# Decode attention on one core: result matmuls placed behind the next tile's first sums, and a first K load in three pieces

## The chip, the cores, the metric

The kernel runs on one core of one Trainium2 chip. The metric is device time in microseconds (us), lower is better; executions of one kernel lay within 0.35% of each other here, except in experiment 7 (0.8%). "V margin" below is my own measure: the time from the issue of a V load to the landing of the load ahead of it in the queue, with landings read from the completion records among the trace's DMA packets (the last of 16 per load). These records are grouped in order of time, which is right as long as the 16 DMA engines drift apart by less than a load lasts. For every whole tile that is so (at most 5.4 us apart in any run, of 19.3 us); for the last small pieces the grouping is rough, except for the very last landing.

## The reference

```python
B, H, Sq, Skv, Dh = 8, 32, 1, 4096, 128          # all bf16
scores = jnp.einsum('bhqd,bhkd->bhqk', q, k) * Dh ** -0.5
attn = softmax(scores, axis=-1)
return jnp.einsum('bhqk,bhkd->bhqd', attn, v)
```

One query per head, 256 heads, K and V of 268 MB each: every byte is read once.

## The kernel before

Eight heads make a tile: 128 partitions by 256 columns (C) by 128 (D), 8.39 MB of K and as much of V, 32 tiles (NT). VectorE multiplies K by the query in four quarters of 64 columns and halves the products once or twice; TensorE sums over what is left of D by matmuls with the identity; VectorE collects the sums as scores and finds the maximum; ScalarE makes the weights; TensorE multiplies them with V in a loop, and `result_of` picks each head's part. K and V share three slots.

```python
kv_pool = ctx.enter_context(tc.tile_pool(name="kv_pool", bufs=SLOTS))     # SLOTS = 3
...
cuts = {                                      # pieces of a load; otherwise one piece
    ("k", 0): [C // 2] * 2,
    ("k", NT - 3): [C // 2] * 2,
    ("k", NT - 2): [C // 2] * 2,
    ("k", NT - 1): [C // 4, C // 4, C // 2],
    ("v", NT - 1): [C // 2, C // 4, C // 8, C // 16, C // 32, LAST, LAST],
}
...                                           # load(): the queries' load follows the first piece of K
def width_of(t, u):
    return D // 4 if u >= NU // 2 and t < NT - 3 else D // 2
...
for t in range(NT):
    loop = 0 < t <= LT                        # LT = NT - 3
    ...
    product(t, 0, Q)                          # VectorE, first quarter
    sum_over_d(t, 0)                          # TensorE
    if t + 1 < NT:
        q_prep(t + 1)
    product(t, Q, 2 * Q)
    sum_over_d(t, 1)
    scores_of(t, 0)                           # VectorE waits here for the first sums
    product(t, 2 * Q, 3 * Q)
    sum_over_d(t, 2)
    scores_of(t, 1)
    ...
    product(t, 3 * Q, C)
    sum_over_d(t, 3)
    scores_of(t, 2)
    if loop:
        values_loop(t - 1)                    # TensorE, some 16 us
        load("k", t + 1)
        load("v", t)
    ...
    scores_of(t, 3)
    weights_of(t)
    ...
    if t > 0:
        copy_of(t - 1)                        # ScalarE, from PSUM
        ...
        if t % R == 0:
            norm_of(n)                        # 1 matmul in the program
        result_of(t - 1)                      # 4 matmuls, need copy_of
```

## Time and profile before

| | before |
|---|---|
| time, median of the runs beside the changed kernel | 1262.24 us (1260.06 to 1263.07) |
| span of the profiled run | 1260.2 us |
| busy: VectorE, TensorE | 83%, 61% |
| VectorE waiting for sums / for K | 106.0 / 72.6 us |

The timeline lists start, length, engine, line, operation, operands, and in brackets the idle time before it and its releaser. This is VectorE over one tile in the middle:

```profile
591.80 4.43 DVE L185 TENSOR_TENSOR kt<-kt,qb 128x8192 bf16<-128x8192 bf16 x1 [2.71 <-DMA kt<-in_k_dram]
...
607.23 0.69 DVE L217 TENSOR_REDUCE sc<-ps 128x64 f32<-128x512 f32 x1 [2.01 <-PE ps L205]
...
626.36 0.69 DVE L217 TENSOR_REDUCE sc<-ps 128x64 f32<-128x512 f32 x1 [1.35 <-PE ps L205]
```

"First sums" are those of a tile's first quarter, "last sums" those of its last. There are two waits that could give: 2.71 us for K, and 2.01 us for the first sums, which TensorE can start only when the loop of the tile before is over.

### The profile page before, as it was taken

Reading aid. Unit: us, or ns where it says so; the run is one execution under the profiler, and the core shown is the slowest. Engines: PE = TensorE matmul, PEld = TensorE weight load, DVE = VectorE, ACT = ScalarE, POOL = GpSimd, SP = SyncE. Lnnn points to the kernel's source line nnn. Section 1 sums busy time; section 2 is a strip of 40 time slices with the busy share of each in tenths; the row PEclk is TensorE's granted clock in tenths of the full one; section 3 lists DMA queues with packets and bytes.
Section 4 is the critical chain, followed back from the end, with each engine's and each line's share of the span. In section 5 each row is a group of like instructions: output and inputs, shape, how many; then the busy total and the mean of one; then the engine's idle time right before and its main releaser. Section 6 shows DMA issues by size and latency. Waiting matters only on the chain. (4 is left out here: it accounts for less than half of the span.)

```text
span 1260.2 us, 11027 instructions
## 1 busy us (share of the span) xinstructions
PE 765.0 (61%) x3067; PEld 287.5 (23%) x3067; DVE 1040.8 (83%) x588; ACT 170.6 (14%) x625; POOL 3.3 (0%) x18
## 2 busy tenths in 40 slices
PE   2265577555776556765567755577555776557756
PEld 0021222211222212222122221222212222212222
DVE  5997988889888888888898888987889888898793
ACT  0111011110111101111011111011110111101111
POOL 0000000000000000000000000000000000000000
PEclk9677887777887778877788777887777887778867
DMA  9999999999999999999999999999999999999997
GB/s 401 433 399 433 433 431 429 410 433 437 435 433 431 425 433 433 433 431 431 431 435 427 433 431 429 433 429 431 433 422 433 433 433 431 433 424 430 429 444 307
DMA packets 11433, 537.33 MB, mean 426 GB/s; under 512 B 1808, under 2 KB 2064, under 8 KB 2320
## 3 DMA queue, kind: packets, MB, share of 16 engines
q1 hardware_dynamic: 11072, 536.94, 99.1%
q8 instruction: 14, 0.23, 0.1%
q10 hardware_dynamic: 336, 0.07, 0.0%
q14 instruction: 11, 0.09, 0.0%
HBM read 536.94 MB, written 0.07 MB: 426 GB/s over the span
## 5 line engine op out<-in xcount | busy, mean ns | idle before, releaser
L185 DVE TENSOR_TENSOR kt<-kt,qb 128x8192 bf16<-128x8192 bf16 x128 | 565.2, 4416 | 84.0 <-DMA kt<-in_k_dram 72.6
L205 PE MATMUL ps<-kt,ident 128*128 128x512 bf16 x792 | 260.3, 479 | 420.1 <-DVE kt L193 370.1
L288 PE MATMUL av<-vt,w 128*32 x1740 | 425.4, 396 | 4.5
L188 DVE TENSOR_TENSOR kt<-kt 128x4096 bf16<-128x4096 bf16 x128 | 293.4, 2292 | 4.4
L288 PEld LDWEIGHTS av<-vt,w 128*32 x1740 | 172.9, 99 | 262.7 <-issue 120.8
L249 ACT ACTIVATE w<-sc,bias 128x256 bf16<-128x256 f32 x256 | 126.4, 494 | 655.4 <-DVE bias L240 655.4
L205 PEld LDWEIGHTS <-ident 128*128 128x128 bf16 x792 | 84.5, 113 | 570.8 <-issue 522.5
L217 DVE TENSOR_REDUCE sc<-ps 128x64 f32<-128x512 f32 x128 | 88.0, 687 | 106.0 <-PE ps L205 106.0
L193 DVE TENSOR_TENSOR kt<-kt 128x2048 bf16<-128x2048 bf16 x58 | 71.0, 1225 | 2.0
L344 ACT ACTIVATE comb<-av 32x512 bf16<-32x512 f32 (+1 forms) x32 | 18.7, 586 | 321.5 <-PEq L278 313.8
L274 PE MATMUL av<-vt,w 128*32 128x512 bf16 x116 | 47.3, 500 | 14.7 <-issue 13.4
L249 ACT ACTIVATION_READ_ACCUMULATOR w<-sc,bias 128x1 f32 x256 | 47.7, 186 | 0.0
L360 PE MATMUL op<-comb,pick 32*16 32x128 bf16 (+1 forms) x128 | 12.1, 213 | 26.0 <-ACT comb L344 26.0
L168 ACT ACTIVATE qg<-qh 8x128 bf16<-8x128 f32 x32 | 8.5, 266 | 99.5 <-PE qh L164 99.5
L274 PEld LDWEIGHTS av<-vt,w 128*32 128x32 bf16 x116 | 6.9, 100 | 55.3 <-issue 55.3
L360 PEld LDWEIGHTS <-pick 32*16 32x16 bf16 (+1 forms) x128 | 8.8, 83 | 33.0 <-issue 32.6
L316 PE MATMUL av<-vt,w 128*32 128x512 bf16 x191 | 15.7, 424 | 0.0
L164 PE MATMUL qh<-q_all,ident 128*8 128x128 bf16 x32 | 7.1, 221 | 13.1 <-DMA q_all<-in_q_dram 13.1
L229 DVE TENSOR_REDUCE pmax<-sc 128x1 f32<-128x256 f32 x32 | 13.5, 421 | 1.1
L170 PE MATMUL qp<-qg,heads 8*128 8x128 bf16 x32 | 6.8, 213 | 11.4 <-ACT qg L168 11.4
L172 ACT ACTIVATE qb<-qp 128x128 bf16<-128x128 f32 x32 | 8.9, 277 | 9.6 <-PE qp L170 9.6
L336 DVE RECIPROCAL rz<-zp 16x1 f32<-16x1 f32 x16 | 2.3, 147 | 7.7 <-PE zp L328 7.7
(29 smaller groups left out, 51.0 us busy)
## 6 DMA issues: line engine op xcount, KB each, us to landing
kt<-in_k_dram SPq DMA_DIRECT2D x7, 4096.0 KB, 21.1
kt<-in_k_dram SPq DMA_DIRECT2D x2, 2048.0 KB, 15.5
vt<-in_v_dram SPq DMA_DIRECT2D x1, 4096.0 KB, 32.1
vt<-in_v_dram SPq DMA_DIRECT2D x1, 2048.0 KB, 36.8
vt<-in_v_dram SPq DMA_DIRECT2D x1, 1024.0 KB, 38.4
vt<-in_v_dram SPq DMA_DIRECT2D x1, 512.0 KB, 39.2
vt<-in_v_dram SPq DMA_DIRECT2D x31, 24.2
kt<-in_k_dram SPq DMA_DIRECT2D x28, 26.6
```

Source lines behind the costliest of these rows:

```text
L185: nc.vector.tensor_tensor(out=part, in0=part, in1=qb[:].to_broadcast([P, MC, D]), op=ALU.mult)
L188: nc.vector.tensor_tensor(out=part[:, :, 0 : D // 2], in0=part[:, :, 0 : D // 2], in1=part[:, :, D // 2 : D], op=ALU.add,)
L193: nc.vector.tensor_tensor(out=part[:, :, 0 : D // 4], in0=part[:, :, 0 : D // 4], in1=part[:, :, D // 4 : D // 2], op=ALU.add,)
L205: nc.tensor.matmul(ps[:], lhsT=ident[:], rhs=kt[:, u * UC : (u + 1) * UC, s * DS : (s + 1) * DS], start=(s == 0), stop=(s == n - 1),)
L217: made = nc.vector.tensor_reduce(out=scs[t][:, u * UC : (u + 1) * UC], in_=sums.pop((t, u))[:], axis=AX.X, op=ALU.add)
L229: nc.vector.tensor_reduce(out=pmax[:], in_=sc[:], axis=AX.X, op=ALU.max)
L249: nc.scalar.activation(out=w[:, :, g, :], in_=sc_g, func=ACT.Exp, bias=bias[:, g : g + 1], scale=scale, accum_out=esum[:, t % R, g : g + 1],)
L274: pe.matmul(av, lhsT=wf[:, i * nw : (i + 1) * nw], rhs=vf[:, i * nv : (i + 1) * nv], **how)
L288: pe.matmul(av, lhsT=wf[:, bass.ds(ow + i * nw, nw)], rhs=vf[:, bass.ds(ov + i * nv, nv)], start=False, stop=False,)
L316: nc.tensor.matmul(avs[t][j * AG : (j + 1) * AG, :], lhsT=w[:, i, :, :], rhs=vt[:, c0 : c0 + CB, :], start=(i < TG), stop=(j not in group[ ...
L344: nc.scalar.activation(out=comb[0:n, :, :], in_=av[0:n, :, :], func=ACT.Copy)
L360: nc.tensor.matmul(ops[n][:], lhsT=pick[0:e, m, r, :], rhs=comb[0:e, m, :], start=(r == 0 and m == 0), stop=(r == R - 1 and m == CB - 1),)
```

## The change

Its intent: the first sums no longer stand behind ScalarE's copy and the results (c); VectorE starts earlier as the queries follow a smaller piece of K (a); and tile 0 needs fewer additions on VectorE (b).

```diff
-        ("k", 0): [C // 2] * 2,
+        ("k", 0): [C // 4, C // 4, C // 2],
@@ width_of
-        return D // 4 if u >= NU // 2 and t < NT - 3 else D // 2
+        return D // 4 if u >= NU // 2 and 0 < t < NT - 3 else D // 2
@@ after sum_over_d(t, 0)
+            if 0 < t - 1 <= LT:
+                if (t - 1) % R == 0:
+                    norm_of(n)
+                if t > 1:
+                    result_of(t - 2)
@@ end of the tile
-                if t % R == 0:
-                    norm_of(n)
-                result_of(t - 1)
+                if not loop:
+                    if t % R == 0:
+                        norm_of(n)
+                    result_of(t - 1)
```

## The prediction

> **What bounds the kernel now.** I read the page of the kernel before in this order: busy shares, the 40 slices, the queues; then the transfer queue's own timeline, a table of stages, VectorE's waits, and the timeline of one tile.
>
> ```profile
> PE 765.0 (61%) x3067; PEld 287.5 (23%) x3067; DVE 1040.8 (83%) x588; ACT 170.6 (14%) x625; POOL 3.3 (0%) x18
> ...
> DMA packets 11433, 537.33 MB, mean 426 GB/s; under 512 B 1808, under 2 KB 2064, under 8 KB 2320
> ```
>
> VectorE is busy 83%, but the kernel must read 537 MB, and the row of DMA digits on the page is 9 in every slice but the last. So the stream of loads is the first suspect, and the question is how near 426 GB/s is to its ceiling. The table of stages says it:
>
> ```profile
> 38.70:77.40 38.70, 11.04 (x26) 3.48 (x26) 36.97 (x20) 4.58 (x18) 0.00 (x0) 0.59 1.00 434
> 77.40:116.10 38.70, 24.07 (x94) 8.93 (x94) 32.63 (x19) 5.17 (x19) 0.00 (x0) 0.81 0.96 407
> 116.10:1122.30 1006.20, 630.67 (x2466) 237.76 (x2466) 844.93 (x480) 137.66 (x507) 0.00 (x0) 0.80 1.00 430
> 1122.30:1238.40 116.10, 73.75 (x308) 27.21 (x308) 99.13 (x55) 15.12 (x56) 0.00 (x0) 0.74 1.00 433
> 80.50:81.90 1.40, 0.95 (x3) 0.13 (x2) 0.91 (x2) 0.00 (x0) 0.00 (x0) 0.50 0.00 0
> ```
>
> The last column is GB/s. The best stretch reaches 434: one tile of 8.39 MB in 19.33 us, a K and a V tile in 38.67. There is one true hole (80.5 to 81.9, nothing moves), and the long middle runs at 430, not 434. At 434 from end to end the kernel would need 1237 us; everything the change can win lies in what is above that: start, hole, middle, tail.
>
> The transfer queue's timeline shows where the hole is from:
>
> ```profile
> 80.95 0.33 SPq L151 DMA_DIRECT2D vt<-in_v_dram  x1
> 97.69 0.33 SPq L151 DMA_DIRECT2D kt<-in_k_dram  x1
> 119.66 0.33 SPq L151 DMA_DIRECT2D vt<-in_v_dram  x1
> 136.57 0.33 SPq L151 DMA_DIRECT2D kt<-in_k_dram  x1
> ```
>
> There are three slots. V(t) reuses the slot of K(t), so it is issued when the last sum of K(t) is done; K(t+2) reuses V(t-1), so it is issued when the loop of tile t-1 ends. From the DMA packets of the trace (their completion records, in order of time) I took when each tile landed. V(1) is issued at 80.95; the tile before it had landed at 80.47: late, hence the hole. After that every V is issued 3.3 to 4.7 us before the previous tile lands, every K 5.5 to 7.5 us before.
>
> VectorE over the whole run, and around one V issue:
>
> ```profile
> DVE sc L217 <- PE ps L205: 106.0, 61, 4.5
> DVE kt L185 <- DMA kt<-in_k_dram: 72.6, 26, 3.9
> DVE kt L185 <- ACT qb L172: 11.4, 1, 11.4
> ```
>
> 26 tiles make VectorE wait for K, about 2.8 us each: the middle is bound by transfers, compute has slack. 31 of the 61 waits for sums are the fixed one at the end of a tile (1.35 us mostly); the others are what the change aims at.
>
> **What the Trainium skill says.** "DMA: Bandwidth & Descriptors", section "Where 436 GB/s comes from", gives 435.2 GB/s as the ceiling of the 16 ports; this trace agrees (434 in the best stages). The same page, "Latency and other measured facts", gives about 0.6 us from a hardware-generated issue to the first byte; here the first packet after the issue at 80.95 starts at 81.90, so 0.95 us, and the first 16 packets took 3.0 to 3.3 us each where others take 2.42. "Runtime: NRT & Kernel Launch", section "Instruction fetch mechanics", says that instructions are refilled in blocks of 16 KiB over DMA and that a taken branch can force a fetch; the trace has 14 transfers of 0.23 MB together on a queue of kind "instruction", about 1 us each on one of the 16 DMA engines. The change keeps loop and branches, so these stay. "TensorE: Matmul & The Clock Gate", section "What's actually happening", says the array runs at half clock after idling; the sums of a tile show it: eight take 3.3 to 3.6 us at PEclk 0.5, 1.90 us right behind a loop.
>
> **The change, part by part.**
>
> *(a) First K load in quarters.* The query tile is issued after the first piece of K. Now that piece is half (4.2 MB, landed at 12.37), the queries landed at 12.64, and VectorE begins at 14.31 (the 11.4 us wait above). With a quarter, half of the piece's 9.67 us of streaming goes: queries at about 7.8, VectorE at 9.4. Gain 4.8 us; cost one more issue of 0.4 us and, as with the quarters of the last K (4.90 + 4.90 against 9.71), 0.1 us of stream. The later half lands at 22.4, when VectorE wants it at about 23.3: no new wait.
>
> *(b) Tile 0 halved once.* Removes two additions of 1.23 us from VectorE (2.4) and adds eight matmuls; the last sum of tile 0 takes 3.4 instead of 1.86, so 1.5 comes back on the path. Net 0.9. Together tile 0 is done 5.7 to 6 us earlier: 40.7 instead of 46.7. But K(1) lands at 41.7 and is usable at 42.2, so tile 1 starts at about 42.4 instead of 48.55, its last sum is done at about 74.8 instead of 80.95, and V(1) is issued 5.6 us before K(2) lands instead of 0.5 late. The hole goes: that tile took 22.70 us instead of 19.33, of which 0.9 is an instruction fetch that stays. **Gain 2.4 us for all later landings.**
>
> *(c) Result and norm behind the first sums.* The order of the built program confirms it: after a loop now come 4 result matmuls (with a norm before them every second tile) and then 8 sums; in the changed kernel 8 sums, norm, 4 results. One tile in the trace:
>
> ```profile
> 96.92 0.61 PE L274 MATMUL av<-vt,w 128*32 128x512 bf16 x2
> 98.33 0.38 PE L360 MATMUL op<-comb,pick 32*16 32x128 bf16 x4 [0.81 <-ACT comb L344]
> 98.64 1.90 PE L205 MATMUL ps<-kt,ident 128*128 128x512 bf16 x8
> ```
>
> The sums start at 98.64 and could start at 97.6, as the loop is done: the copy by ACT (0.59), its semaphores and four matmuls (0.31) leave VectorE's path, 1.0 to 1.1 us per tile. Nothing is added: ACT's copy then lies beside the sums, and the results (0.4 us) come before sums that VectorE needs some 8 us later.
>
> In the middle this is not on the bound. It becomes margin: the wait for the first sums averages 1.7 us there; if they come 1.05 earlier the V load is issued 1.05 earlier, the next loop too, and the wait falls again until it is zero. So V margins rise from about 4.1 to 4.1 + 1.7 = 5.7 us or so. Does margin help? I compared, from the packets, the mean landing of the 16 engines from tile to tile: K tiles (margins 6 to 7.5) take 19.34, V tiles (margins 3.3 to 4.7) 19.6 on average and up to 20.5; in the first 5 us after a V issue packets are stretched by up to 1.8 us, after a K issue by nothing. The one V with a margin of 5.3 took 19.35. Summed over 26 V tiles that is about 6.5 us, in agreement with 430 against 434 over 1006 us (9 us, fetches included). If margin is the cause, most of it goes; I count **4.5 us**, as an estimate, since the slowest engine and not the mean decides and fetches still spread the engines.
>
> *(d) The tail.* From tile 29 on, K comes in halves, VectorE no longer waits for loads, and the chain that ended last runs from 1187 on through VectorE:
>
> ```profile
> 1187.73 0.59 ACT comb L344
> 1188.33 0.04 issue
> 1188.37 0.38 PE op L360 x4
> 1188.75 1.85 PE ps L205 x8
> ```
>
> Here (c) is direct: tiles 28, 29 and 30 give 1.0 to 1.1 each, 3.2 in all. But V(31) limits it: its last piece landed at 1254.12, two microseconds before the last value matmul was done (1256.3). With data alone as the bound, its second half of matmuls (4.7 us now, twelve of them one behind another) would end at about 1254.1. **Gain 2.2 us**; the 3.9 us of copy, result, scale and store after it stay.
>
> Sum: 2.4 + 4.5 + 2.2 = 9.1 us; 1262.1 - 9.1 = **1253.0 us**.
>
> **The rivals.**
> *The stretched packets have nothing to do with margin* (memory or instruction fetches): for it, fetches do lie in some slow tiles, and V issues always fall where ACT and TensorE start; against it, K issues are clean. Then only 2.4 + 2.2 are won: 1257.5.
> *The hole is merely moved*: a faster start gives the time back at the next wait, or the quarters cost more in the start than they give. Speaks against it: the stream is idle only there. Then only the tail is won: about 1260.
> *All stretch goes and the engines stay together*: 2.4 + 6.5 + 2.2, 1251; with part of the instruction fetches absorbed too, 1249.5.
> *A new wait*: the results now sit ahead of the query matmuls and the next sums; one scratch tile between copy and result, one PSUM tile for the result. All have a whole tile of slack; I give it 3%.
>
> **Range and chances.** 1253.0, with 1249.5 to 1257.5 from the second and third lines of the rivals. A gain over 2% needs under 1237, the time of the pure stream: 1%. Slower by 2%: 1%. Within 2%: 98%.
>
> **What would show it.** Right: VectorE's first product near 9.4; V(1) issued near 75 and no stage at 407; the wait for sums down from 106 to about 60 us or less, and the wait for K up by about as much; the middle at 432 to 434; the final chain no longer through VectorE's products of tile 30 but ending behind the last V pieces. Wrong: V margins of 5.5 us or more with the middle still at 430 (then stretch is not from late issue); or waits for sums unchanged; or a new wait of PE on the copy.

## The result

The changed kernel takes 1253.45 us (1253.05 to 1254.02, 4 runs) against 1262.24 us (4 runs): a ratio of 0.9933, 95% interval 0.9916 to 0.9951. All ratios here are formed from fast runs; they are not quite the ratios of the medians. It is 8.8 us faster and clear of noise.

The stages of the changed kernel, the same windows as before. The columns are the window and its length, busy time and number of instructions of TensorE, its weight loads, VectorE, ScalarE and GpSimd, then the granted clock, the DMA share and GB/s:

```profile
77.40:116.10 38.70, 24.83 (x97) 9.35 (x96) 32.64 (x18) 5.74 (x22) 0.00 (x0) 0.81 1.01 434
116.10:1122.30 1006.20, 627.52 (x2464) 235.01 (x2462) 847.57 (x476) 137.00 (x505) 0.00 (x0) 0.79 1.00 433
```

The stage with the hole went from 407 to 434, the middle from 430 to 433. The transfer queue's timeline:

```profile
75.37 0.33 SPq L151 DMA_DIRECT2D vt<-in_v_dram  x1
92.16 0.33 SPq L151 DMA_DIRECT2D kt<-in_k_dram  x1
113.44 0.33 SPq L151 DMA_DIRECT2D vt<-in_v_dram  x1
```

V(1) is issued at 75.37, 5.1 us ahead of the landing of K(2), instead of 0.5 late. VectorE's waits (us in total, times, longest):

```profile
DVE kt L185 <- DMA kt<-in_k_dram: 98.9, 22, 5.9
DVE sc L217 <- PE ps L205: 56.6, 34, 3.6
DVE kt L185 <- ACT stage L369: 17.4, 4, 4.4
...
DVE kt L185 <- ACT w L249: 4.2, 1, 4.2
```

The wait for sums lost 49 us. The wait before a tile's first product gained 48: the rows put down to ACT are of the same length as those for K and stand at the same instruction, and a wait for several semaphores is put down to the one that came last by the profile, so I count them as waits for K (98.9 + 17.4 + 4.2 = 120.5 against 72.6). In the middle the wait for the first sums is gone, and K alone is waited for:

```profile
586.26 4.42 DVE L185 TENSOR_TENSOR kt<-kt,qb 128x8192 bf16<-128x8192 bf16 x1 [4.42 <-DMA kt<-in_k_dram]
...
599.59 0.69 DVE L217 TENSOR_REDUCE sc<-ps 128x64 f32<-128x512 f32 x1
```

TensorE after a loop:

```profile
91.39 0.60 PE L274 MATMUL av<-vt,w 128*32 128x512 bf16 x2
92.19 1.89 PE L205 MATMUL ps<-kt,ident 128*128 128x512 bf16 x8 [0.19 <-PEq L278]
94.00 0.39 PE L360 MATMUL op<-comb,pick 32*16 32x128 bf16 x4
```

The sums start 0.80 us after the loop's last matmuls start, where they started 1.72 us after before: 0.92 us came off. And the chain that ended last now ends in loads:

```profile
1201.69 40.81 DMA vt<-in_v_dram
1242.50 0.04 issue
1242.54 5.49 PE av L316 x29
...
1248.11 0.60 ACT comb L344
```

Where the 8.3 us between the two spans (1260.2 and 1251.9) came from, by landings:

| | before | after | gained | forecast |
|---|---|---|---|---|
| start, to the landing of K(3) | 123.41 | 120.63 | 2.8 | 2.4 |
| middle, K(3) to V(27) | 994.55 | 990.35 | 4.2 | 4.5 |
| V(27) to the last piece of V(31) | 136.16 | 136.10 | 0.1 | 0 |
| last landing to the end of the span | 6.1 | 4.8 | 1.2 | 2.2 |

### The profile page after: what moved, and what is told of

Same layout as the page of the kernel before. It is cut to its first block, busy times and chain, and to the rows that moved or that the text cites. A ratio compares the mean times of both kernels' runs of the same rounds, so it can differ in the third digit from the quotient of the medians.

```text
span 1251.9 us, 11042 instructions
## 1 busy us (share of the span) xinstructions
PE 767.1 (61%) x3075; PEld 286.0 (23%) x3075; DVE 1036.0 (83%) x586; ACT 170.6 (14%) x625; POOL 3.3 (0%) x18
## 5 line engine op out<-in xcount | busy, mean ns | idle before, releaser
L185 DVE TENSOR_TENSOR kt<-kt,qb 128x8192 bf16<-128x8192 bf16 x128 | 565.3, 4416 | 127.2 <-DMA kt<-in_k_dram 98.9
L316 PEld LDWEIGHTS <-w 128*32 128x32 bf16 x191 | 6.8, 105 | 11.0 <-issue 7.2
```

The source lines that it names most:

```text
L185: nc.vector.tensor_tensor(out=part, in0=part, in1=qb[:].to_broadcast([P, MC, D]), op=ALU.mult)
L316: nc.tensor.matmul(avs[t][j * AG : (j + 1) * AG, :], lhsT=w[:, i, :, :], rhs=vt[:, c0 : c0 + CB, :], start=(i < TG), stop=(j not in group[ ...
```

## The experiments

Each time stands beside runs of the kernel before on the same chip, whose median was 1261.76 us for the first four, 1261.98 for the next four and 1262.11 for the last four. "Middle" is the time from the landing of K(3) to that of V(27), "period" the median time from one V issue to the next from V(2) on; both, like the margins, are of the profiled run. All twelve kernels gave correct results.

| | time us | ratio | V margin, median | period | middle |
|---|---|---|---|---|---|
| before | 1262.24 | 1 | 4.12 | 38.92 | 994.55 |
| changed | 1253.45 | 0.9933 | 5.67 | 38.76 | 990.35 |
| 1 order only | 1255.86 | 0.9952 | 5.69 | 38.70 | 990.21 |
| 2 start only | 1256.68 | 0.9958 | 4.30 | 38.90 | 991.06 |
| 3 without (b) | 1253.12 | 0.9932 | 5.68 | 38.75 | 990.39 |
| 4 margin another way | 1254.32 | 0.9942 | 6.93 | 38.69 | 989.68 |
| 5 1.2 us off the cycle | 1253.93 | 0.9938 | 4.44 | 38.74 | 990.50 |
| 10 1.6 us off the cycle | 1257.46 | 0.9960 | 4.08 | 38.77 | 993.60 |
| 6 2.4 us off the cycle | 1266.82 | 1.0041 | 3.73 | 39.01 | 1002.50 |
| 7 3.7 us off the cycle | 1281.65 | 1.0161 | 3.27 | 39.83 | 1015.04 |
| 8 1.2 us in the cycle | 1260.14 | 0.9985 | 4.37 | 39.03 | 995.87 |
| 9 changed, again | 1253.40 | 0.9929 | 5.70 | 38.76 | 990.33 |
| 11 tail groups | 1253.43 | 0.9930 | 5.69 | 38.74 | 990.37 |
| 12 tail pieces | 1253.72 | 0.9933 | 5.68 | 38.75 | 990.50 |

My theory going in was the prediction's: the middle is bound by the stream of loads, and it runs at 430 instead of 434 GB/s because V loads are issued only about 4 us ahead ("margin theory"). Rivals: the slow packets are unrelated to margin; the start gives everything.

### 1. Only the order

The kernel before with part (c) alone; the edit is the last two hunks of the diff above.

> Only the new place of the result and norm matmuls; start as before. My theory (the hole is from the start, the stretched packets in the middle from V loads issued only about 4 us ahead, the tail from the last V pieces): the hole at 80 us stays, V(1) issued near 80.9; the wait for first sums goes to about zero after a few tiles and V margins rise to 5.6 us, the middle goes from 430 to 433 GB/s; end gains 4.5 (middle) + 1.3 (tail) = about 5.8 us, 1256.5 us, ratio about 0.9955. Rival (stretch has nothing to do with margin, the 7 us came from the start): only the tail is gained, 1.3 to 2 us, about 1260.5 us, ratio 0.9988.

Measured: 1255.86 us, 5.9 us gained where 5.8 were expected. V(1) is still issued at 80.91, the hole stays, and the middle is as in the changed kernel (990.21). The rival without a role for margin (1260.5) is out.

### 2. Only the start

```diff
-        ("k", 0): [C // 2] * 2,
+        ("k", 0): [C // 4, C // 4, C // 2],
-        return D // 4 if u >= NU // 2 and t < NT - 3 else D // 2
+        return D // 4 if u >= NU // 2 and 0 < t < NT - 3 else D // 2
```

> Only the start: first K in quarter, quarter, half, and tile 0 halved once; results stay ahead of the sums. My theory: V(1) issued near 75.4 as in the changed kernel, hole gone, 2.4 us gained; from tile 2 on V margins fall back to about 4 us because the first sums are late again, so the middle stays at 430 GB/s: about 1259.8 us, ratio 0.998. Rival (start gives it all): about 1255 us, ratio 0.994. Second rival (the gain is given back): 1262, ratio 1.000.

Measured: 1256.68 us. That is 5.1 us gained, twice what my theory gave, and with the 5.9 of the first experiment it makes more than both together give (8.8). The V issues show why, here V(3) and V(7):

```profile
153.44 0.33 SPq L151 DMA_DIRECT2D vt<-in_v_dram  x1
...
309.29 0.33 SPq L151 DMA_DIRECT2D vt<-in_v_dram  x1
```

The four steps average 38.96 us, as in the kernel before (38.97 over 25 steps), while the loads ahead of them landed every 38.76 us (159.04 to 314.09): hardly anything was stretched and the margin was comfortable. So in the order of before something else beats at 38.9 us: a cycle. The loop waits for the last sums of tile t, these for the second half of VectorE's work, that for the collected first sums, these for the first sums on TensorE, and those, in that order, for results, copy and the loop of the tile before. A K that lands earlier doesn't shorten it. The better start gave a head start: the margin was 5.6 us at V(3) and fell, in steps of 0.1 to 0.4 with one rise, to 3.7 us at V(13). The V issues kept it all: from V(1) to V(28) they lie 5.2 to 6.0 us before those of the kernel before. The landings caught up with them while the stream ran clean: 2.2 us earlier at V(1), 5.2 us at V(10). That is where the unexpected 2.7 us came from. It is also why the two parts overlap: with (c) the stream and no longer the cycle sets the pace, and a head start is then worth only what it saves the stream (2.8 us).

From here on I had a second theory, the "cycle theory": the cycle alone made the middle slow, and small margins were only its trace.

### 3. Without the halving of tile 0

The changed kernel with `t < NT - 3` restored in `width_of`.

> The changed kernel with tile 0 halved twice in its second half as before (so without part b). My working: tile 0 is done 0.6 to 0.9 us later, V(1) issued near 76, still over 4 us before K(2) lands, so no hole and later margins the same: time equal to the changed kernel within 0.3 us, 1253.5 us, ratio 0.993. If part b had carried the gain at the start: 1255 or more.

Measured: 1253.12 us, the same. V(1) is issued at 76.17 instead of 75.37 and still 4.3 us ahead. Part (b) does what it should, 0.8 us, and buys nothing once (a) and (c) are there.

### 4. Margin by another way

The kernel before, nothing moved; VectorE saves one addition in the third quarter of a tile, TensorE has four more sums.

```diff
-        return D // 4 if u >= NU // 2 and t < NT - 3 else D // 2
+        return D // 4 if u >= (NU // 2 + 1 if t > 0 else NU // 2) and t < NT - 3 else D // 2
```

> The kernel before with nothing moved, but the third quarter of tiles 1 to 28 also halved once: VectorE saves one addition of 1.2 us per tile, TensorE gets four more matmuls that lie beside VectorE's next product. Another way to issue V loads earlier. Margin theory: V margins rise from 4.1 to about 5.5 us or more, the middle goes to 433 GB/s, hole also goes as tile 1 is 1.2 us shorter (V(1) at 79.7, so partly: some 1.2 of 2.4 us): gain 4.5 + 1 = 5.5 us, about 1256.5, ratio 0.9955. Rival (stretch is not from margin; the gain in the changed kernel's middle is from the moved matmuls themselves): gain of 1 us at most, 1261, ratio 0.999.

Measured: 1254.32 us, 7.4 us gained, even better than forecast. So nothing is special about moving the matmuls: another microsecond taken off the same path does it too. The experiment can't tell the two theories apart, as the third quarter lies in the cycle too.

### 5 to 7. Later V loads, off the cycle

The changed kernel with idle work for VectorE in tiles 2 to 26, between the first and second quarter. That is before VectorE takes up the first sums, so the path from these sums to the next loop isn't lengthened, and only the V issue moves.

```diff
             product(t, 0, Q)
             sum_over_d(t, 0)
+            if 2 <= t <= LT - 3:
+                for _ in range(1):            # 2 and 3 in the next two
+                    nc.vector.tensor_reduce(
+                        out=idle[:], in_=loads["k", t][:, 0:8, :].rearrange("p c d -> p (c d)"),
+                        axis=AX.X, op=ALU.max,
+                    )
```

> The changed kernel with one idle VectorE reduction (about 1.2 us by the rate of its neighbours) in tiles 2 to 26, between the first and the second quarter of a tile: every V load is issued 1.2 us later, margin 5.65 -> about 4.4 us, as before the change. It lies in time in which VectorE would wait for K, and not between the first sums and the next loop. Margin theory, as in the prediction (a V load issued only about 4 us ahead costs stream time): the middle falls back towards 430 GB/s, 3 to 4.5 us lost, about 1257 us. Cycle theory, formed after the second experiment (the middle before was set by the cycle loop - copy - results - first sums - second half of VectorE's tile - last sums - loop, 38.96 us, over the stream's 38.70, and small margins with stretched packets were only its trace): nothing lost, 1253.5 us within 0.5.

Measured: 1253.93 us, 0.5 us lost at a median margin of 4.44 us. The six runs go from 1253.03 to 1257.01 us, so this loss is not clear of noise. The cycle theory had it right.

> The same with two such reductions: margin about 3.2 us, smaller than anywhere before the change. Margin theory: at least as slow in the middle as before, 1258 us or more. Cycle theory: still nothing or little, 1253.5 to 1254.5 us, though packets of the engines that run ahead are stretched after each V issue.

Measured: 1266.82 us, 13 us lost. Here the cycle theory is plainly wrong and the margin theory right: with V issues 3.2 to 3.6 us ahead in half of the tiles, the stream loses time although VectorE still waits for K (70.2 us in all) and the wait for sums is unchanged (58.1 us).

> The same with three: margin about 2.0 us. The engines that run 2 to 4 us ahead of the slowest now run dry at every V load, the slowest not yet. Margin theory: well over 1262 us (25 tiles by 0.5 us or more on top of before). Cycle theory: as the slowest engine sets a landing, 1254 to 1257 us.

Measured: 1281.65 us. Again the margin theory, by far. (The five runs go from 1277.19 to 1287.30 us; the profiled one took 1278.05 us, so the margin and the middle in the table are those of a quick run. Its median margin was 3.27 us, not the 2.0 us expected.) My argument that only the engines that run ahead would starve is refuted: the landing of the slowest engine suffers too.

### 8. The same microsecond, in the cycle

The same reduction once, placed after `scores_of(t, 1)`, between the third and fourth quarter.

> The same single reduction of 1.2 us, in the same tiles, but between the third and the fourth quarter, so within the cycle. It delays V loads by the same 1.2 us at first. Cycle theory: the cycle goes from 37.9 to 39.1 us, above the stream's 38.70; V issues come every 39.1 us, the margin of 5.65 is used up at 0.4 us per tile and then the middle runs at 39.1: some 25 x 0.4 less about 1.7 of used margin, 8 to 9 us lost, about 1262 us. Margin theory: the same as the single reduction off the cycle, about 1257 us, V issues every 38.7 to 38.9 us.

Measured: 1260.14 us, 6.7 us lost, against 0.5 us for the same instruction off the cycle. V issues now come every 39.03 us, as the cycle theory said (39.1); the loss is somewhat under its 8 to 9 us. In 20 of tiles 2 to 27 VectorE again waits for the first sums, up to 1.5 us; in experiment 5 it did so in one, for 0.4 us. In the trace the instruction takes 1209 ns here and 1220 ns off the cycle:

```profile
L413 DVE TENSOR_REDUCE idle<-kt x25: 1208/1209/1209, 103.5 to 1042.9; 128x1 f32<-128x1024 bf16 x25
```

### 9 and 10. The margin of before, without its cycle

First the changed kernel again, as the neighbour of the last three.

> The changed kernel itself, on the chip of the three runs beside it, to compare with them: 1253.5 us within 0.5, ratio to before 0.993.

Measured: 1253.40 us. Then the reduction off the cycle with 11 columns (`0:11` for `0:8`).

> The idle reduction off the cycle again, now of 11 columns (about 1.6 us): margins near 4.0 us, what the kernel before had. No loss at 4.4 us (0.5 us), 13 us lost at 3.2: this dose tells whether margins of the kernel before are by themselves costly. If the cycle alone made the middle before slow: 1253.5 to 1254.5 us. If a margin of 4.0 alone costs what the middle lost before: 1257 to 1258 us, and the two causes hold each other up there.

Measured: 1257.46 us; 4.1 us lost. The reduction's row, and below it the stage table for the middle of this kernel:

```profile
L401 DVE TENSOR_REDUCE idle<-kt x25: 1619/1620/1621, 87.8 to 1023.8; 128x1 f32<-128x1408 bf16 x25
```

```profile
116.10:1085.00 968.90, 607.20 (x2372) 228.42 (x2371) 851.68 (x484) 132.28 (x487) 0.00 (x0) 0.79 1.00 431
```

431 GB/s; the same window gives 431 in the kernel before and 433 in the changed one. With a median margin of 4.08 us (before: 4.12) and a cycle that is short (no wait for the first sums in tiles 2 to 27), the middle loses 3.3 us against the changed kernel, where the kernel before loses 4.2. So a margin of 4.1 is costly by itself.

### 11 and 12. The tail

The forecast for the tail was the one term that was clearly off. In the last tile twelve value matmuls share one column group; this spreads them:

```diff
-            0 if t == NT - 1 and C // 2 <= c0 < C // 2 + 3 * C // 16 else c0 // CB % TG
+            c0 // CB % TG
```

> The changed kernel, with the value matmuls of the last tile all spread over four column groups (now twelve of them share one group and run one behind another). The data-bound tail that I forecast: last value matmul about 2 us earlier than now (1246 instead of 1248), the last piece of V (landed at 1247.1) then sets the end: 0.8 to 1.2 us gained, 1252.5 us. If TensorE at half clock makes four groups slow too: nothing gained.

Measured: 1253.43 us, nothing gained. TensorE in its tail:

```profile
1242.34 1.04 PE L316 MATMUL av<-vt,w 128*32 128x512 bf16 x16 [2.21 <-DMA vt<-in_v_dram]
1244.84 1.04 PE L316 MATMUL av<-vt,w 128*32 128x512 bf16 x8 [1.45 <-DMA vt<-in_v_dram]
1246.05 1.58 PE L316 MATMUL av<-vt,w 128*32 128x512 bf16 x7 [0.17 <-DMA vt<-in_v_dram]
1247.37 0.58 PE L354 MATMUL op<-vt,w_last 128*16 128x128 bf16 x4
1248.37 0.59 PE L360 MATMUL op<-comb,pick 128*16 128x128 bf16 x4 [0.42 <-ACT comb L344]
```

The matmuls are quick now but wait for each piece of V, and the last value matmul ends at 1247.6, against 1248.2 in the run beside it; the last results take 0.59 instead of 0.38 us. The profiled spans differ by 0.5 us (1251.7 and 1252.2), the medians not at all.

> That, and the last V load in five pieces instead of seven (128, 64, 32, 28 and 4 columns): the pieces of 8 and 4 columns take about 0.7 to 1.0 us each in the stream where their bytes need 0.6 and 0.3. Last landing 0.7 us earlier, another 0.5 us gained: 1252.0 us. If fewer pieces let the last matmuls begin too late: the same as the run beside it.

(The edit, on top of that of experiment 11: `[C // 2, C // 4, C // 8, C // 8 - LAST, LAST]` for the last V.) Measured: 1253.72 us, nothing gained; the last piece lands at 1246.87, as beside it (1246.89). Fewer pieces did not bring the last landing forward. I didn't find a version that beats the changed kernel.

## Why the prediction was right, and where its steps were not

- *Time.* 1253.0 forecast, 1253.45 measured, and the sum has nearly the right parts: start 2.8 for 2.4, middle 4.2 for 4.5, tail 1.2 for 2.2.
- *(a) and (b), the start.* VectorE's first product starts at 9.61 (forecast 9.4), V(1) is issued at 75.37 (forecast 74.8), the hole is gone. That (b) is dispensable follows from the prediction's own terms (0.9 us, with over 4 us in hand), and experiment 3 shows it. What the prediction missed is that an early start alone would be kept through a middle that is paced by the issues (experiment 2: 5.1 us and not 2.4).
- *(c), one tile.* Forecast 1.0 to 1.1 us, measured 0.92. The wait for the first sums did go to zero and V margins did rise to 5.7 us, as forecast.
- *(c), the middle: number right, half of the mechanism.* The step "26 tiles make VectorE wait for K ... the middle is bound by transfers, compute has slack" failed. The wait for K lies before the first quarter, and in the order of before what came after was held up by the first sums anyway: the kernel before waits for them in every one of tiles 3 to 27, for 0.65 to 2.6 us (1.7 on average), and the changed kernel in none. Around that wait ran a cycle of 38.9 us, longer than the 38.70 us of a K and a V tile. Experiment 2 shows the cycle running at its own pace while loads were early; experiment 8 shows that 1.2 us put into the cycle costs 6.7 us where the same 1.2 us beside it costs 0.5. The other half, "does margin help?", held: experiments 5, 10, 6 and 7 delay the V issue without lengthening the cycle and lose 0.5, 4.1, 13 and 28 us. That 4.5 came so near to 4.2 is in part luck: it was set by judgement below a stretch read as 6.5 us (the prediction's own averages, 26 times 19.6 less 19.34, give 6.8), and that stretch was the stream following the cycle.
- *How the two fit.* In the kernel before, the cycle set the pace: since VectorE waited for the first sums after every wait for K, a K landing later by less than that second wait would have delayed nothing after it. With a cycle longer than the stream's period, V issues slip back against the stream tile by tile (0.2 us per tile in experiment 2), until the margin is so small that loads slow down by as much as the cycle is too long. The kernel before sat at that point: a margin of 4.1 us. Removing 0.9 us made the cycle shorter than the stream, the margin grew to where VectorE's own chain puts it, 5.7 us, and the loss went. But a short cycle alone would not have been enough: with the margin held at 4.1 us the middle loses 3.3 of the 4.2 us without any cycle (experiment 10). The change removed both at once. This account fits experiments 1 to 10. Why loads slow down when the next one is issued under some 4.4 us ahead is not shown by these runs.
- *(d), the tail.* The step that was mis-sized: "With data alone as the bound, its second half of matmuls ... would end at about 1254.1", that is, with the last landing. They ended 0.95 us after it (1248.03 and 1247.08), so 1.2 and not 2.2 us were gained. The rest isn't to be had by regrouping matmuls (experiment 11) or by fewer pieces (experiment 12): then TensorE waits for one piece after another.
- *Rivals.* "The stretched packets have nothing to do with margin" is refuted by experiments 5 to 7 and 10; "the hole is merely moved" by the table of landings; a new wait of TensorE on the copy did not come (the results at 94.00 wait for nothing).
- *Slips that cost nothing.* 32 and not 31 of the 61 waits for sums are those at the end of a tile. The range of 1249.5 to 1257.5 comes from the first and the third rival, not from the second and the third; the 1260 of the second lay outside it.

## What to carry to other kernels

A wait for loads does not prove that a kernel is bound by loads: compare the period of the issues with the period of the stream, and if the issues come slower even where loads are early, look for a cycle through the engines and cut that. When a kernel streams at the ceiling, count how far ahead each load is issued, not only whether the queue is empty. And test with the same small delay in two places, on and off the suspected path, in several doses: one dose had told the wrong story here.

## What the Trainium skill lacked or had wrong

- "DMA: Bandwidth & Descriptors" (section "Rules for kernel authors") says to issue a load early, and "Latency and other measured facts" gives about 0.6 us to the first byte; none of its sections says how far ahead a load has to be issued to keep a saturated queue full. Here, for loads of 8.39 MB from one queue and against a margin of 5.7 us, 25 tiles with 4.4 us lost 0.5 us in all (not clear of noise), with 4.1 us 4.1, with 3.7 us 13 and with 3.3 us 28 (medians of the V margins; K margins averaged 6.6 us or more). An empty queue took 0.95 us to its first packet.
- The same page (section "iDMA fabric — 4 AXI ports for 8 engines, asymmetric across TPBs") says, in a passage that it marks as unconfirmed, that a bulk load runs at the pace of its slowest engine; no page says how far the 16 engines drift apart in a long stream. In the changed kernel the completions of one load were 0.4 us apart at K(2) and 4.1 us at K(31).
- "Perfetto Trace Analysis" (section "What \"DMA-bound\" means") names the DMA engines, the issuing sequencer and SBUF read capacity as bounds of such a kernel; it doesn't say that one whose loads hardly pause can still be paced by its engines. Here it was, by a cycle through TensorE, ScalarE and VectorE of 38.9 us against 38.70 us of stream, at 430 of 434 GB/s.
